# A two-layer attention block with less work ahead of its main loop: one place of maxima and two groups of queries moved

## The chip, the cores and the metric

The kernel runs on one core of a Trainium2 chip. The metric is the device time in microseconds of one execution, the median of several. A profiled execution of the same kernel gives the page and the trace that are read below. The engines are TensorE (PE; its weight load is listed as PEld), VectorE (DVE), ScalarE (ACT), GpSimd (POOL) and SyncE (SP), which here issues nearly all DMAs. Each engine works through its own instructions in order; they wait for each other by semaphores.

## The reference

All numbers are float32; one batch, S = 2048 rows, D = 512 columns, 32 query heads of 16 and a single head of keys and values:

```
mod = silu(c) @ w_mod                       # six rows of 512: sa, ca, ga, sb, cb, gb
h = layernorm(x) * (1 + ca) + sa
q = h @ wq  (32 heads of 16);  k = h @ wk;  v = h @ wv    # one head of k, v
p = softmax(q k^T / 4);  o = p v
x = x + ga * (o @ wo)
h = layernorm(x) * (1 + cb) + sb
out = x + gb * (relu(h @ w1) @ w2)          # w1: 512 x 1792, w2: 1792 x 512
```

The softmax is exact in form: the maximum of each row of scores is subtracted. The weights are scaled so that scores are large, and the matrix products are built from a rounded high part and a remainder where one rounded product isn't exact enough.

## The kernel before, in words

**Blocks, groups, units.** Rows of queries are handled in eight blocks of 256; the 32 heads in four groups of eight. A block and a group are a unit: 32 units, u = block * 4 + group. A unit's scores against all 2048 keys come in sixteen steps of 128 keys (`scores`, L723, with four tiles `ct` 0 to 3), each a matmul of 50 rows: 48 hold a head's queries and keys in high and low parts, the last two hold minus the row's maximum, high and low part, against rows of ones in `kp`. So a unit's scores can't be formed before its maxima are known and stand in those two rows. `values` (L847) multiplies the exponentials with the values; the sum of the exponentials comes along as another column.

**Maxima.** `max_of` (L417) forms 512 scores for 128 queries (L426) and VectorE reduces them (L428); there are 64 such for each unit, eight to a "place". After a unit's last one, VectorE reduces the four results a row (L432), turns them (L392), ScalarE and GpSimd split them (`split`, L239), SyncE writes them to DRAM in four DMAs (L399) and loads them in four others, one for each `ct`, into rows 48 and 49 of the unit's queries (L405).

**The head and the first loop (L794 to L828).** The first block of 512 rows of x is normalised and transposed, with the modulation's rows sa and ca; group 0 of the queries is formed (`qproj_now`, L803), written to DRAM in a layout of heads (L339) and loaded for unit 0 (`load_q`, L368, its DMAs at L376). Blocks of 512 are normalised in the order `ln1_sums` (L268: mean and variance), `ln1` (L273: the reciprocal root by VectorE in about 14 small operations, then the rows by GpSimd and ScalarE), `tr1` (L286: transposes, and the writes of `hT` with scale and shift) and `kv` (L302: keys and values). Then the first loop takes NBITS = 43 steps: in each, two or three maxima of those in `first_max`, and one step of the generator `first` (L653), which holds the rest of transposes, keys and values, queries of groups 1 and 2, and four modulation rows. `first_max` has the 64 maxima of unit 0 and LEAD / 8 = 3 places, 24 maxima, of unit 1. The constants NBITS and LEAD are written by hand.

**The main loop (L859 to L902).** 256 chunks, eight to a unit. The letters of PARTS (L40) give the order on TensorE in each chunk's two halves: `c` and `d` are scores (d is already of the next step, so that the first d of a unit stands in the second half of the chunk before it), `a` and `b` maxima of one place, `u` and `l` the two halves of a portion of other work on the other half of the array, `t` transposes; after each half the values. In a chunk the instructions are given out in this order: the letters; at position 3 of the first half what was put off (`put_off`: splits and their DMAs, among them L399); with the last `l` the next portion is fetched (`advance`), and whatever the generator does between two portions is issued there, its DMAs too; at the end what is due (`ends`: L405 among them) and a step of `chores` (loading and splitting weights, chunks 0 to 34).

The portions come from `queries` (L674: groups 3 to 13 of the sixteen products of 512 rows by 128 columns, three portions each) and then, block by block of 32 chunks, from `behind` (L511) for the block that is finished: rest of the second layer of the block before (7 portions for one half of the rows), projection, second norm, first layer in 14 portions with its weights loaded two ahead into three buffers `w1s` (L450, DMA L452), second layer. Finished rows go out by L533. In block 0, where no second layer is waiting yet, queries 14 and 15 and four empty portions stand in its place. An empty portion is filled with six matmuls whose result nobody reads (L873 to L876).

Where a place ends up in time: chunk c takes the place c + LEAD / 8 of those from unit 1 on. With three places ahead, the maxima of unit u end in chunk 8u - 4, L399 is issued in chunk 8u - 3 and L405 at that chunk's end; the first scores of unit u are in the second half of chunk 8u - 1. `load_q` of the next unit is issued when a unit has 16 maxima left (L421).

Of the kernel before, what the change touches and what calls it, by code (L numbers as in the profile page):

```python
# [9 lines left out]
F32 = mybir.dt.float32  # L10
F32R = mybir.dt.float32r
I32 = mybir.dt.int32
AF = mybir.ActivationFunctionType
OP = mybir.AluOpType
# [5 lines left out]
P = 128  # L20
LB = 512
NL = S // LB
TB = 256
# [4 lines left out]
NG = 4  # L28
# [2 lines left out]
NU = NB * NG  # L31
EPS = 1e-5
HP = 64
NBITS = 43
LEAD = 24
ET = mybir.EngineType


# [18 lines left out]
def build(tc, nc, cst, sb, ps, dr, x, wq, wk, wv, wo, w1, w2, c, w_mod, out):  # L57
# [21 lines left out]
    wm, xb1 = {}, {}  # L79
# [34 lines left out]
    cols = cst.tile([P, 2, DC], F32, name="cols")  # L114
# [7 lines left out]
    qdr = [[dr.tile([8, 48, LB], F32R, name=f"qdr{b}_{j}") for j in range(NG)] for b in range(NL)]  # L122
# [83 lines left out]
    def ln_sums(mv, t, src):  # L206
        st = sb.tile([P, 6], F32, name="st", tag="st", bufs=2)
        nc.vector.bn_stats(st, src)  # L208
        nc.vector.bn_aggr(mv[:, t], st)

    def ln_mv(n):
        return sb.tile([P, n, 2], F32, name="mv", tag="mv", bufs=2)

    def ln_stats(mv, n, late):
        nm = sb.tile([P, n], F32, name="nm", tag="nm", bufs=2)
        ve = sb.tile([P, n], F32, name="ve", tag="ve", bufs=2)
        y = sb.tile([P, n], F32, name="y", tag="y", bufs=2)
        u = sb.tile([P, n], F32, name="u", tag="u", bufs=2)
        yi = y.bitcast(I32)
        nc.vector.tensor_scalar(ve, mv[:, :, 1], EPS, None, op0=OP.add)  # L220
        nc.vector.tensor_scalar(yi, ve.bitcast(I32), 1, None, op0=OP.logical_shift_right)
        nc.vector.tensor_scalar(yi, yi, -1.0, float(0x5f3759df), op0=OP.mult, op1=OP.add)
        if late:
            for _ in range(3):
                nc.vector.tensor_tensor(u, y, y, op=OP.mult)
                nc.vector.scalar_tensor_tensor(u, u, -0.5, ve, op0=OP.mult, op1=OP.mult)
                nc.vector.scalar_tensor_tensor(y, u, 1.5, y, op0=OP.add, op1=OP.mult)
            nc.vector.tensor_scalar(nm, mv[:, :, 0], -1.0, None, op0=OP.mult)
            return nm, y
        nc.gpsimd.tensor_scalar(nm, mv[:, :, 0], -1.0, None, op0=OP.mult)  # L230
        for _ in range(3):
            nc.gpsimd.tensor_tensor(u, y, y, op=OP.mult)
            nc.gpsimd.tensor_tensor(u, u, ve, op=OP.mult)
            nc.gpsimd.tensor_scalar(u, u, -0.5, 1.5, op0=OP.mult, op1=OP.add)
            nc.gpsimd.tensor_tensor(y, y, u, op=OP.mult)
        return nm, y
# [28 lines left out]

    ln = {}

    def ln1_sums(b):  # L268
        ln[b] = ln_mv(4)
        for t in range(4):  # L270
            ln_sums(ln[b], t, xb1[b][:, t])

    def ln1(b):  # L273
        xb = xb1[b]
        nm, y = ln_stats(ln[b], 4, True)
        nmy = sb.tile([P, 4], F32, name="nmy", tag="nmy", bufs=2)
        nc.vector.tensor_tensor(nmy, nm, y, op=OP.mult)
        for t in range(4):
            if t < 2:
                nc.gpsimd.tensor_scalar(xb[:, t], xb[:, t], nm[:, t:t + 1], y[:, t:t + 1],  # L280
                                        op0=OP.add, op1=OP.mult)
            else:
                nc.scalar.activation(xb[:, t], xb[:, t], AF.Identity,
                                     bias=nmy[:, t:t + 1], scale=y[:, t:t + 1])

    def tr1(b):  # L286

        xb = xb1[b]
        h = hT[b] = sb.tile([P, DC, LB], F32, name="hT", tag="big", bufs=4)
        for k in range(DC):  # L290
            pt = ps_exp()
            for t in range(4):
                nc.tensor.transpose(pt[:, t * P:(t + 1) * P], xb[:, t, k * P:(k + 1) * P], idn)  # L293
            if b == 0 and k % 2:
                nc.vector.tensor_scalar(h[:, k], pt, cols[:, 1, k:k + 1], cols[:, 0, k:k + 1],
                                        op0=OP.mult, op1=OP.add)
            else:
                nc.scalar.activation(h[:, k], pt, AF.Identity,
                                     bias=cols[:, 0, k:k + 1], scale=cols[:, 1, k:k + 1])
            yield  # L300

    def kv(b):  # L302
# [26 lines left out]
    def qproj(b, j, bank, soon=False, qq=None):  # L329


        pt = bank()
        todo = [("f32", pt[:, n:n + TB], wqf[j][:, k], hT[b][:, k, n:n + TB],
                 n + k == 0, n + k == TB + DC - 1)
                for n in range(0, LB, TB) for k in range(DC)]

        def to_dram(qq):
            for r, part in ((0, 0), (32, 0), (16, 1)):
                nc.sync.dma_start(qdr[b][j].bitcast(F32)[:, r:r + 16], qq[:, part].bitcast(F32))  # L339

        def end():
            qt = qq if qq is not None else sb.tile([P, 2, LB], F32R, name="qq", tag="t4", bufs=2)
            if soon:
                nc.scalar.activation(qt[:, 0], pt, AF.Copy, scale=DH ** -0.5)
                nc.vector.scalar_tensor_tensor(qt[:, 1], pt, DH ** -0.5, qt[:, 0].bitcast(F32),
                                               op0=OP.mult, op1=OP.subtract)
                to_dram(qt)
                return
            stg = sb.tile([P, 512], F32, name="stg", tag="tmp", bufs=2)
            put_off.append(split_psum(qt[:, 0], qt[:, 1], pt, stg=stg, scale=DH ** -0.5))  # L350
            put_off.append(partial(to_dram, qt))

        return todo, end

    def qproj_now(*args):

        todo, end = qproj(*args)
        for n in range(0, len(todo), 2):
            on_all(todo[n])
            on_all(todo[n + 1])  # L360
            if n + 2 == len(todo):
                end()
            yield
# [4 lines left out]
    def load_q(u):  # L368
        b, g = divmod(u, NG)
        tb, to = divmod(b * TB, LB)  # L370
        qps[u] = []
        for i in range(2):
            t = sb.tile([P, 2, TB], F32R, name="qp", tag="qp", bufs=6)
            for hf in range(2):
                h0 = (i * 2 + hf) * 2
                nc.sync.dma_start(  # L376
                    t[hf * 64:hf * 64 + 48].bitcast(F32),
                    qdr[tb][g].bitcast(F32)[h0:h0 + 2, :, to:to + TB].rearrange("h r n -> r h n"))
            qps[u].append(t.rearrange("p a n -> p (a n)"))
# [37 lines left out]
    def max_of(u, hf, i, j, kb):  # L417
# [12 lines left out]
        if left[u] == 0:  # L430
# [9 lines left out]
                  for kb in range(KB) for hf in (1, 0)]  # L440
    places = places[LEAD // 8:]

# [68 lines left out]
    def behind(b):  # L511
# [23 lines left out]
        x1, oo = open_block(b)  # L535
        if b == 0:
            qqs = [sb.tile([P, 2, LB], F32R, name="qq", tag="w1s", bufs=3) for _ in range(2)]
            rest, fill = [others_of(14 + n, qqs[n]) for n in range(2)]
            fill = itertools.chain(fill, [[]] * 4)
        else:  # L540
            rest, fill = carried.pop(), second(b - 1, 1)
        yield next(rest)
# [5 lines left out]
        mv = ln_mv(TT)  # L548
        for t in range(TT):
            pt = ps_fill()  # L550
# [22 lines left out]
        for f2 in range(FC // 2):  # L573
            pt = ps_fill()
# [4 lines left out]
            i, f = divmod(f2 * 2, 8)  # L579
# [73 lines left out]
    def first():  # L653

        mods = [mod_all(i, dst, (ps_fill, ps_exp)[n % 2]) for n, (i, dst) in
                enumerate(((2, gr[:, 0]), (5, gr[:, 1]), (3, sbr), (4, cbr)))]
        yield from kvs[1]
        for b in range(2, NL):
            yield from trs[b]
            yield from kvs[b]  # L660
        yield from qproj_now(0, 1, ps_exp, True)
        load_q(1)
        for m in mods:
            yield from m
        yield from qproj_now(0, 2, ps_fill, True)

    def others_of(n, qq=None):

        todo, end = qproj(*divmod(n, NG), ps_fill, qq=qq)
        for i in range(0, len(todo), 3):  # L670
            yield todo[i:i + 3]
        end()

    def queries():  # L674
        for n in range(3, 14):
            yield from others_of(n)

    def chores():
# [106 lines left out]
    def run(g):  # L785
        for _ in g:
            pass
# [4 lines left out]
    kvs = [kv(b) for b in range(NL)]  # L792

    warm(32)  # L794
    ln1_sums(0)
    row1 = mod_row(1, ps_max())
    ln1(0)
    row0 = mod_row(0, ps_max())
    mod_col(row1, 1, True, ps_max())
    mod_col(row0, 0, False, ps_max())  # L800
    run(trs[0])
    ln1_sums(1)
    run(qproj_now(0, 0, ps_exp, True))  # L803
    ln1(1)
    load_q(0)
    for i in (2, 5, 3, 4):
        load_mod(i)
    for _ in range(DC):
        next(kvs[0])
    ln1_sums(2)  # L810
    run(trs[1])
    ln1(2)
    ln1_sums(3)
    next(kvs[0])
    for _ in range(DC):
        next(kvs[1])
    ln1(3)

    bits, done = first(), 1
    upto = [len(first_max) * n // NBITS for n in range(NBITS + 1)]  # L820
# [38 lines left out]
    for c in range(NU * KT // 2):  # L859
# [5 lines left out]
        if places:  # L865
            u, i, j = places.pop(0)
            todo_of.update(a=[partial(max_of, u, 0, i, j, kb) for kb in range(KB)],
                           b=[partial(max_of, u, 1, i, j, kb) for kb in range(KB)])
# [4 lines left out]
        if not portion:  # L873

            pt = ps_fill()
# [60 lines left out]
```

## Time and profile before

| what | us |
|---|---|
| median of three runs | 1703.93 |
| the three runs | 1693.88, 1703.93, 1709.46 |
| the profiled execution | 1703.82 |
| its span | 1702.0 |
| head, to the first reduce of a maximum | 41.09 |
| first scores of unit 0 | 109.77 |
| sum of unit 0 copied out | 159.11 |
| sum of unit 31 copied out | 1620.77 |

Times in a trace are counted from the start of the span. A row of the timeline has the start, the duration, the engine (a trailing q means its sequencer, which is where DMAs are issued), the line, the operation, what it writes and reads, and how many instructions were merged into the row; in brackets stands how long the engine was idle before it, and what ended that. The granted clock is TensorE's, as a share of full speed. "Busy" of TensorE is modelled in part, since matmuls are pipelined.

### The profile page before, as it was taken

The page shows a single profiled execution, that of the slowest core. Times are in us where ns is not written, and L with a number is a line of the kernel's source. Part 1 is how long each engine was busy: PE and PEld are TensorE (multiplying, and loading weights), DVE is VectorE, ACT ScalarE, POOL GpSimd, SP SyncE. Part 2 cuts the span into 40 slices and gives each one's busy share as a digit, 9 for nine tenths or more (in the row PEclk, how much of TensorE's full clock was granted, in tenths as well). Part 3 has the DMA queues.
Part 4 walks back from the last instruction along what each step waited for, and adds up shares of the span by engine and source line. Part 5 has one row for each costly group of instructions (what it writes and reads, how often), then busy time and mean ns, then how long its engine had stood idle before and what let it go on. Part 6 is the DMA issues. An engine that isn't in the chain of part 4 may idle for free.

```text
span 1702.0 us, 34026 instructions
## 1 busy us (share of the span) xinstructions
PE 1669.9 (98%) x13130; PEld 923.7 (54%) x13130; DVE 1374.6 (81%) x2347; ACT 1227.2 (72%) x2397; POOL 345.9 (20%) x434
## 2 busy tenths in 40 slices
PE   7999999999999999999999999999999999999988
PEld 5444444445654565546644565446644565456567
DVE  7788888888889888888889888888888888886031
ACT  4238888877877777778777787778877787778810
POOL 3103345331102211131113110131113110131110
PEclk9899999999999999999999999999999999999999
DMA  8024643212211131103201131103211230113133
GB/s 284 31 62 142 193 126 108 88 56 91 91 29 35 47 114 40 60 16 109 78 29 47 56 100 35 58 16 119 68 35 41 67 108 29 48 35 103 44 103 111
DMA packets 86928, 129.86 MB, mean 76 GB/s; under 512 B 25012, under 2 KB 52596, under 8 KB 86768
## 3 DMA queue, kind: packets, MB, share of 16 engines
q1 hardware_dynamic: 85184, 127.62, 24.2%
q8 instruction: 105, 1.72, 0.4%
q14 instruction: 55, 0.45, 0.1%
q10 hardware_dynamic: 1584, 0.07, 0.1%
HBM read 100.33 MB, written 25.15 MB: 74 GB/s over the span
## 4 chain that ended last, share of the span: by engine, by line
PE 93%; DVE 3%; DMA 2%; ACT 1%; issue 1%; POOL 0%; SPq 0%; POOLq 0%; DVEq 0%; ACTq 0%
PE ps_pv L853 30%; PE ps_exp L727 21%; PE ps_fill L163 19%; PE ps_max L426 18%; PE ps_exp L146 1%; PE ps_max L146 1%; DVE pm L428 1%; DMA w1s<-w1dr 1%; PE ps_exp L307 1%; DVE st L208 1%; PE ps_exp L293 0%; PE ps_exp L190 0%; DMA wmod<-in_w_mod_dram 0%; PE ps_exp L159 0%; PE ps_fill L190 0%
## 5 line engine op out<-in xcount | busy, mean ns | idle before, releaser
L428 DVE TENSOR_REDUCE pm<-ps_max 128x1 f32<-128x512 f32 x2048 | 1292.7, 684 | 189.6 <-PE ps_max L426 141.8
L729 ACT ACTIVATE pe<-ps_exp 128x512 f32<-128x512 f32 x2048 | 1081.2, 605 | 301.5 <-PE ps_fill L163 140.2
L426 PE MATMUL ps_max<-kp,qp 48*128 48x512 f32 x2048 | 805.1, 439 | 7.2 <-DVE pm L428 7.1
L727 PE MATMUL ps_exp<-qp,kp 50*128 50x512 f32 x2048 | 723.0, 412 | 1.9 <-ACT pe L729 1.8
L853 PE MATMUL ps_pv<-pe,vt 128*32 128x512 f32 x4096 | 545.5, 605 | 0.0
L426 PEld LDWEIGHTS ps_max<-kp,qp 48*128 48x128 f32 x2048 | 363.9, 185 | 264.7 <-DVE pm L428 237.4
L727 PEld LDWEIGHTS ps_exp<-qp,kp 50*128 50x128 f32 x2048 | 358.8, 185 | 269.1 <-ACT pe L729 177.9
L163 PE MATMUL ps_fill<-w2r,r 64*128 64x512 f32 x1044 | 302.7, 405 | 0.0
L163 PE MATMUL ps_fill<-hh,w1s 64*128 64x256 f32 x1568 | 243.1, 286 | 0.0
L163 PEld LDWEIGHTS ps_fill<-hh,w1s 64*128 64x128 f32 x1568 | 217.1, 186 | 12.9 <-PEq L156 6.7
L163 PEld LDWEIGHTS ps_fill<-w2r,r 64*128 64x128 f32 x1044 | 180.6, 185 | 11.8 <-PEq L156 2.5
L853 PEld LDWEIGHTS ps_pv<-pe,vt 128*32 128x32 f32 x4096 | 80.5, 108 | 142.3 <-issue 122.0
L163 PE MATMUL ps_fill<-hT,wq 64*128 64x256 f32 x416 | 128.3, 405 | 0.0
L241 POOL TENSOR_TENSOR r<-stg,r 128x512 fp32r<-128x512 f32 x49 | 62.9, 1283 | 322.1 <-ACT r L240 322.1
L163 PE MATMUL ps_fill<-hl,w1s 64*128 64x256 f32 x784 | 126.3, 280 | 0.0
L163 PEld LDWEIGHTS ps_fill<-hl,w1s 64*128 64x128 f32 x784 | 105.5, 185 | 0.0
L163 PEld LDWEIGHTS ps_fill<-hT,wq 64*128 64x128 f32 x416 | 68.3, 185 | 2.9
L897 POOL TENSOR_TENSOR on<-num,den 128x256 f32<-128x256 f32 x31 | 22.8, 736 | 231.2 <-DMA den<-recs 192.3
L743 POOL COPY num<-pvs 128x256 f32<-128x256 f32 x32 | 12.8, 398 | 179.4 <-ACT pvs L739 179.4
L241 POOL TENSOR_TENSOR hl<-stg,hh 128x512 fp32r<-128x512 f32 x14 | 18.0, 1284 | 131.3 <-ACT hh L240 131.3
L261 POOL TENSOR_TENSOR x<-stg,x 128x512 f32<-128x512 f32 x14 | 18.1, 1290 | 99.1 <-ACT stg L260 99.1
L248 ACT ACTIVATE stg<-ps_fill 128x512 f32<-128x512 f32 x62 | 38.2, 616 | 0.0
(139 smaller groups left out, 929.6 us busy)
## 6 DMA issues: line engine op xcount, KB each, us to landing
w1s<-w1dr SPq DMA_DIRECT2D x112, 512.0 KB
qdr<-qq SPq DMA_DIRECT2D x48, 256.0 KB
qp<-qdr SPq DMA_DIRECT2D x128, 96.0 KB
raw<-in_B_w_dram SPq DMA_DIRECT2D x28, 256.0 KB
w1dr<-w1s SPq DMA_DIRECT2D x14, 512.0 KB
wmod<-in_w_mod_dram SPq DMA_DIRECT2D x6, 1024.0 KB
x<-in_A_x_dram SPq DMA_DIRECT2D x8, 512.0 KB
out_dram<-ot SPq DMA_DIRECT2D x16, 256.0 KB
```

What stands on the lines that cost most here:

```text
L146: nc.tensor.matmul(pt, w, a, start=start, stop=stop)
L163: ins = nc.tensor.matmul(pt, w[r], a[r], start=start and h == 1, stop=stop and h == 0)
L208: nc.vector.bn_stats(st, src)
L241: (eng or nc.gpsimd).tensor_tensor(lo, src, hi.bitcast(F32), op=OP.subtract)
L248: nc.scalar.activation(stg, pt, func, **kw)
L261: nc.gpsimd.tensor_tensor(dst, stg, other, op=OP.add)
L426: nc.tensor.matmul(pt, qps[u][i][r, j * P:(j + 1) * P], kp[r, kb * 512:(kb + 1) * 512], start=True, stop=True)
L428: nc.vector.tensor_reduce(pms[u][:, (i * 2 + hf) * 4 + j, kb:kb + 1], pt, axis=AX.X, op=OP.max)
L727: nc.tensor.matmul(pt, kp[r, kt * P:(kt + 1) * P], qps[u][ct // 2][r], start=True, stop=True)
L729: nc.scalar.activation(pe, pt, AF.Exp)
L853: nc.tensor.matmul(pvt[i * 32:(i + 1) * 32], vt[:, kt], pes.pop((s, i)), start=(kt == 0), stop=(kt == KT - 1))
L897: due[1]()
```

## The change

Queries of group 1 (of the first 512 rows) are formed before the first loop and no longer in it, those of group 2 in the main loop, as the first of `queries`. Queries 11 move from `queries` to block 0 of `behind`, where they, 14 and 15 now leave one empty portion of four; 14 and 15 share one buffer. The first loop has 35 steps, and two places ahead, 80 maxima in all, 16 of unit 1. Queries formed early are written in two halves of columns, and the first half is loaded (`load_q`) before the second is written. The sums for blocks 1 to 3 stand earlier in the program, the statistics of blocks 2 and 3 are formed in one chain of operations on 8 columns, and all four writes of the first transposed block are by ScalarE. With two places ahead, the maxima of unit u end in chunk 8u - 3.

```diff
-NBITS = 43
-LEAD = 24
+NBITS = 35
+LEAD = 16
...
-    def ln1_sums(b):
-        ln[b] = ln_mv(4)
+    def ln1_sums(b, mv, n=0):
+        ln[b] = mv, n
         for t in range(4):
-            ln_sums(ln[b], t, xb1[b][:, t])
-
-    def ln1(b):
-        xb = xb1[b]
-        nm, y = ln_stats(ln[b], 4, True)
-        nmy = sb.tile([P, 4], F32, name="nmy", tag="nmy", bufs=2)
+            ln_sums(mv, n + t, xb1[b][:, t])
+
+    def ln1_stats(mv, n):
+        nm, y = ln_stats(mv, n, True)
+        nmy = sb.tile([P, n], F32, name="nmy", tag=f"nmy{n}", bufs=2)
         nc.vector.tensor_tensor(nmy, nm, y, op=OP.mult)
+        return nm, y, nmy
+
+    def ln1(b, nm, y, nmy):
+        xb, n = xb1[b], ln[b][1]
...
-            if b == 0 and k % 2:
-                nc.vector.tensor_scalar(h[:, k], pt, cols[:, 1, k:k + 1], cols[:, 0, k:k + 1],
-                                        op0=OP.mult, op1=OP.add)
-            else:
-                nc.scalar.activation(h[:, k], pt, AF.Identity,
-                                     bias=cols[:, 0, k:k + 1], scale=cols[:, 1, k:k + 1])
+            nc.scalar.activation(h[:, k], pt, AF.Identity,
+                                 bias=cols[:, 0, k:k + 1], scale=cols[:, 1, k:k + 1])
...
-        def to_dram(qq):
+        def to_dram(qq, cols=slice(0, LB)):
             for r, part in ((0, 0), (32, 0), (16, 1)):
-                nc.sync.dma_start(qdr[b][j].bitcast(F32)[:, r:r + 16], qq[:, part].bitcast(F32))
+                nc.sync.dma_start(qdr[b][j].bitcast(F32)[:, r:r + 16, cols],
+                                  qq[:, part, cols].bitcast(F32))
...
-                to_dram(qt)
+                to_dram(qt, slice(0, TB))
+                load_q(b * LB // TB * NG + j)
+                to_dram(qt, slice(TB, LB))
...
-            rest, fill = [others_of(14 + n, qqs[n]) for n in range(2)]
-            fill = itertools.chain(fill, [[]] * 4)
+            rest, *fill = [others_of(n, qqs[n > 11]) for n in (11, 14, 15)]
+            fill = itertools.chain(*fill, [[]])
...
-        yield from qproj_now(0, 1, ps_exp, True)
-        load_q(1)
         for m in mods:
             yield from m
-        yield from qproj_now(0, 2, ps_fill, True)
...
-        for n in range(3, 14):
+        for n in (*range(2, 11), 12, 13):
             yield from others_of(n)
...
     run(trs[0])
-    ln1_sums(1)
+    ln1_sums(1, mv[1])
+    stats1 = ln1_stats(mv[1], 4)
     run(qproj_now(0, 0, ps_exp, True))
-    ln1(1)
-    load_q(0)
+    ln1(1, *stats1)
     for i in (2, 5, 3, 4):
         load_mod(i)
     for _ in range(DC):
         next(kvs[0])
-    ln1_sums(2)
+    for b in (2, 3):
+        ln1_sums(b, mv[2], (b - 2) * 4)
     run(trs[1])
-    ln1(2)
-    ln1_sums(3)
     next(kvs[0])
+    stats23 = ln1_stats(mv[2], 8)
+    ln1(2, *stats23)
     for _ in range(DC):
         next(kvs[1])
-    ln1(3)
+    ln1(3, *stats23)
+    run(qproj_now(0, 1, ps_exp, True))
```

More of the change, by code (lines that the diff above doesn't have):

```diff
@@ L211, in ln_mv @@
     def ln_mv(n):
-        return sb.tile([P, n, 2], F32, name="mv", tag="mv", bufs=2)
+        return sb.tile([P, n, 2], F32, name="mv", tag=f"mv{n}", bufs=2)
     def ln_stats(mv, n, late):
[L215 to L218, printed above, removed]
+        nm = sb.tile([P, n], F32, name="nm", tag=f"nm{n}", bufs=2)
+        ve = sb.tile([P, n], F32, name="ve", tag=f"ve{n}", bufs=2)
+        y = sb.tile([P, n], F32, name="y", tag=f"y{n}", bufs=2)
+        u = sb.tile([P, n], F32, name="u", tag=f"u{n}", bufs=2)
         yi = y.bitcast(I32)
@@ L266, in build @@
     ln = {}
-    def ln1_sums(b):
-        ln[b] = ln_mv(4)
+    def ln1_sums(b, mv, n=0):
+        ln[b] = mv, n
         for t in range(4):
-            ln_sums(ln[b], t, xb1[b][:, t])
-    def ln1(b):
-        xb = xb1[b]
-        nm, y = ln_stats(ln[b], 4, True)
-        nmy = sb.tile([P, 4], F32, name="nmy", tag="nmy", bufs=2)
+            ln_sums(mv, n + t, xb1[b][:, t])
+    def ln1_stats(mv, n):
+        nm, y = ln_stats(mv, n, True)
+        nmy = sb.tile([P, n], F32, name="nmy", tag=f"nmy{n}", bufs=2)
         nc.vector.tensor_tensor(nmy, nm, y, op=OP.mult)
+        return nm, y, nmy
+    def ln1(b, nm, y, nmy):
+        xb, n = xb1[b], ln[b][1]
         for t in range(4):
+            one = slice(n + t, n + t + 1)
             if t < 2:
-                nc.gpsimd.tensor_scalar(xb[:, t], xb[:, t], nm[:, t:t + 1], y[:, t:t + 1],
+                nc.gpsimd.tensor_scalar(xb[:, t], xb[:, t], nm[:, one], y[:, one],
                                         op0=OP.add, op1=OP.mult)
@@ L283, in ln1 @@
                 nc.scalar.activation(xb[:, t], xb[:, t], AF.Identity,
-                                     bias=nmy[:, t:t + 1], scale=y[:, t:t + 1])
+                                     bias=nmy[:, one], scale=y[:, one])
     def tr1(b):
@@ L794, in build @@
     warm(32)
-    ln1_sums(0)
+    mv = [ln_mv(4), ln_mv(4), ln_mv(8)]
+    ln1_sums(0, mv[0])
     row1 = mod_row(1, ps_max())
-    ln1(0)
+    ln1(0, *ln1_stats(mv[0], 4))
     row0 = mod_row(0, ps_max())
```

## The prediction

> **What bounds the kernel now.** Read first the page's busy shares, then its chain that ended last, then the stages:
>
> ```profile
> PE 1669.9 (98%) x13130; PEld 923.7 (54%) x13130; DVE 1374.6 (81%) x2347; ACT 1227.2 (72%) x2397; POOL 345.9 (20%) x434
> PE 93%; DVE 3%; DMA 2%; ACT 1%; issue 1%; POOL 0%; SPq 0%; POOLq 0%; DVEq 0%; ACTq 0%
> 41.09:59.00 17.91, 17.18 (x39) 7.09 (x39) 11.47 (x20) 4.64 (x6) 1.52 (x2) 0.52 0.19 72
> 59.00:109.78 50.78, 50.04 (x168) 21.47 (x167) 45.12 (x76) 10.59 (x18) 5.31 (x5) 1.00 0.08 25
> 109.78:1561.00 1451.22, 1445.40 (x11933) 784.44 (x11933) 1267.21 (x2103) 1139.66 (x2241) 310.84 (x384) 1.00 0.24 71
> ```
>
> TensorE is the chain nearly everywhere. In the main loop (from 109.78) it is busy 1445.40 of 1451.22 us, so a pause put into its queue there lengthens the run by its own length. The first loop (41.09 to 109.78) is different: its first 18 us ran at a granted clock of 0.52. So two questions decide: what the first loop loses, and whether TensorE must wait in the main loop for something that now comes later.
>
> **The first loop.** Rows of the timeline, and one stage (its columns are the busy time of TensorE, its weight load, VectorE, ScalarE and GpSimd, then granted clock, DMA share and GB/s):
>
> ```profile
> 36.38 0.17 DVE L220 TENSOR_SCALAR ve<-mv 128x4 f32<-128x4 f32 x1
> 41.09 1.28 DVE L428 TENSOR_REDUCE pm<-ps_max 128x1 f32<-128x512 f32 x2
> 61.26 6.06 DVE L428 TENSOR_REDUCE pm<-ps_max 128x1 f32<-128x512 f32 x10
> 87.68 1.29 DVE L428 TENSOR_REDUCE pm<-ps_max 128x1 f32<-128x512 f32 x2 [0.19 <-PE ps_max L426]
> 110.51 0.69 DVE L345 SCALAR_TENSOR_TENSOR qq<-ps_fill,qq 128x512 fp32r<-128x512 f32 x1 [0.19 <-ACT qq L344]
> 109.77 0.96 PE L727 MATMUL ps_exp<-qp,kp 50*128 50x512 f32 x3
> 16.70 1.65 ACT L298 ACTIVATE hT<-ps_exp,cols 128x512 f32<-128x512 f32 x2 [1.18 <-PE ps_exp L293]
> 18.02 3.70 PE L146 MATMUL ps_exp<-hT,wq 128*128 128x256 f32 x16
> 31.71 5.35 PE L307 MATMUL ps_exp<-hT,wkv 128*128 128x512 f32 x8
> 38.50:41.91 3.41, 0.20 (x2) 0.09 (x1) 3.34 (x6) 1.44 (x3) 3.16 (x4) 1.00 1.05 387
> 22.38 2.06 SPq L339 DMA_DIRECT2D qdr<-qq  x3
> 29.93 1.76 SPq L376 DMA_DIRECT2D qp<-qdr  x4
> ```
>
> It ran 68.7 us, from the first maxima (41.09) to the first scores (109.77). A step with two maxima and two passes of 512 columns takes 1.29 + 0.19 = 1.48 us at full clock; a step of transposes is bound by its maxima, 6.06 / 5 = 1.2. After: 35 steps, 80 maxima, so ten steps have three. Those cost three reduces, 1.94. The sum: 8 steps of transposes (two of them with three maxima) 11.4; 3 short ones that turn the values 4; 24 others (eight with three) 39. That is 54.4, and 0.3 for the end of unit 0. VectorE alone would need 80 x 0.645 + 1 = 52.6, so 54.7 is no wild figure.
>
> Its start: the head loses one whole chain of norm statistics (some 14 small operations; the last chain held VectorE from 36.38 to 41.09) since blocks 2 and 3 share one, 8 wide at the same small price. It gains queries of group 1 in front of the loop: 3.70 us of TensorE. ScalarE takes over two of the first four writes of the transposed block, 0.83 each, which makes the first queries some 0.7 us later. Keys of block 1 then start at about 30.9 instead of 31.71, half of them at the lower clock as in the row of 5.35; they end at about 36.8, the queries at 40.5, their copy (0.6) and subtraction (0.69) at 41.8. First maxima at 41.8 against 41.09: +0.7, between -2 and +4 by how the clock stands. But TensorE now works from 31 to 41, where it was busy for 0.20 of the 3.41 us from 38.50, so I expect full clock in the loop. First scores at 41.8 + 54.7 = 96.5 against 109.77: **-13.3** (-9 to -17).
>
> The first exponentials then no longer queue behind the copy of group 2, nor its bank behind the subtraction at 110.51: **-0.7**. Writing the first queries in halves moves a load of q (it waited from 24.4 to 29.93 for the write to land) ahead of three more writes and of the four loads of modulation; each takes SyncE's queue about 2 us. These are hidden: q is first needed by the maxima at 41, and the modulation only after the keys of two more blocks. Without that cover it would cost those 2 us. Buffer tags per width cost nothing: memory, no instruction.
>
> **The main loop, without waits.** One place of eight maxima moves here. Ends of units (copy of the values' sum):
>
> ```profile
> 1435.79 0.60 ACT L739 ACTIVATE pvs<-ps_pv 128x512 f32<-128x512 f32 x1 [0.29 <-PE ps_pv L853]
> 1482.45 0.64 ACT L739 ACTIVATE pvs<-ps_pv 128x512 f32<-128x512 f32 x1
> 1576.94 0.60 ACT L739 ACTIVATE pvs<-ps_pv 128x512 f32<-128x512 f32 x1
> 1620.77 0.60 ACT L739 ACTIVATE pvs<-ps_pv 128x512 f32<-128x512 f32 x1 [3.01 <-PE ps_pv L853]
> ```
>
> A unit of eight chunks with maxima took 46.66, the last one, without, 43.83: 0.35 a place. Three portions of queries replace three of filler; no row prices the difference alone, so 0 to 1.0 (as if each were a place), and I take 0.35, near the lower end because both feed the same half of the array. Together **+0.7**.
>
> **The waits that appear.** A place less ahead means that each unit's maxima end one chunk (5.8 us, 46.66 / 8) later, while its scores stay where they are. The path: maxima, split, four writes to DRAM (L399), four loads (L405) into the queries, first scores. For unit 10:
>
> ```profile
> 573.52 1.70 SPq L399 DMA_DIRECT2D mdr<-ms  x4
> 576.37 1.13 SPq L405 DMA_DIRECT2D qp<-mdr  x4
> 583.52 0.36 SPq L533 DMA_DIRECT2D out_dram<-ot  x1
> 583.92 3.44 SPq L452 DMA_DIRECT2D w1s<-w1dr  x2
> 585.43 0.39 PE L727 MATMUL ps_exp<-qp,kp 50*128 50x512 f32 x1
> DMA  0000029999794787988995220000000969475889
> ```
>
> Before, L405 was issued 9.06 us before the unit's first scores (585.43). Shifted by 5.8, 3.2 remain; a 4 KB transfer lands about 1.5 after its issue (the last of the four writes goes out at about 574.8, and 576.37 waits for it), so where nothing else stands in SyncE's queue all is in time, with a microsecond to spare. But in the new chunk the finished rows (L533) and the first-layer weights (L452) are issued ahead of L405: the program fetches the next portion before it runs what is due. L405 then goes out from 584.3, and its packets stand behind 256 and 512 KB. The last line is the DMA engines' share in 40 slices of 0.15 us from 583.5: busy until slice 24, 587.1. So the load of ct 1 lands at about 587.6 and that of ct 3 at 588.1, where the scores want them at 585.43 and 0.23 later: 2.4 us. TensorE's queue is in order; values, maxima, fill and with them ScalarE and VectorE stand behind. The same place comes once in each block of four units: 10, 14, 18, 22, 26, 30. **+14.4** (0 if the chunk has slack that I don't see, 18 if DMA is slower).
>
> Units 1, 4 and 6 meet the write of queries (L339, 256 KB) instead:
>
> ```profile
> 239.40 2.94 SPq L339 DMA_DIRECT2D qdr<-qq  x3
> 242.43 2.42 SPq L399 DMA_DIRECT2D mdr<-ms  x4
> 247.04 1.43 SPq L405 DMA_DIRECT2D qp<-mdr  x4
> 149.49 2.36 SPq L339 DMA_DIRECT2D qdr<-qq  x3
> 156.38 0.39 PE L727 MATMUL ps_exp<-qp,kp 50*128 50x512 f32 x1
> 293.21 2.94 SPq L339 DMA_DIRECT2D qdr<-qq  x3
> 300.10 0.39 PE L727 MATMUL ps_exp<-qp,kp 50*128 50x512 f32 x1
> 390.00 1.28 POOL L241 TENSOR_TENSOR hl<-stg,hh 128x512 fp32r<-128x512 f32 x1 [5.16 <-ACT hh L240]
> 396.77 0.39 PE L727 MATMUL ps_exp<-qp,kp 50*128 50x512 f32 x1
> ```
>
> Unit 3 shows this meeting already: 4.7 us from the end of L339 (242.34) to L405, 1.2 to the last of its four, 1.5 to land. After, it moves to the chunks of units 1 and 4: 151.85 + 7.4 = 159.3 against 156.6, and 296.15 + 7.4 = 303.5 against 300.3. **+2.7** and **+3.2**. Unit 6: the last queries (15) are now split in the chunk of L399, behind the split at 390.00; written out by about 393.2, landed 5.5 later (as 24.4 to 29.93), and only then may the weights' load take their buffer and L405 follow: after 398.7 + 3 against 396.77: **+5** (2 to 7). The third queries themselves (read back a chunk after their write) have two microseconds to spare; 0 to +2, I take 0. Waits together: **+25.3**.
>
> **The clock.** Stages around low work:
>
> ```profile
> 24.84:28.26 3.42, 1.63 (x9) 0.89 (x8) 3.21 (x12) 2.61 (x5) 1.52 (x2) 1.00 0.51 187
> 1642.76:1646.17 3.41, 1.83 (x9) 1.23 (x7) 2.30 (x13) 0.00 (x0) 1.17 (x2) 1.00 0.00 0
> 1646.17:1649.59 3.42, 0.98 (x7) 0.74 (x7) 0.00 (x0) 0.58 (x2) 2.12 (x2) 1.00 0.21 77
> 1649.59:1653.00 3.41, 3.34 (x15) 3.34 (x16) 1.29 (x2) 0.51 (x2) 0.00 (x0) 0.50 0.00 0
> ```
>
> A stretch of 3.4 us with 0.98 busy was followed by one at 0.50, one with 1.83 was not; 1.63 (mostly transposes) was, as the keys' slow row shows. A pause of 2.4 leaves 1.0 of a stretch if it lies wholly within it, so some pauses will bring the half clock: I take five of the nine, one stretch each, 1.7 lost: **+8.5** (0 to 30; the slow stage at 41.09 lasted five stretches).
>
> [...]
>
> **Sum.** -13.3 - 0.7 + 0.7 + 25.3 + 8.5 = +20.5. The profiled execution took 1703.82 (span 1702.0), the median of the runs shown is 1703.93: **1725**.
>
> **Rivals.**
> [...]
> - No waits: if the loads of maxima pass in time (their order or size lets them overtake the 512 KB), the shorter first loop is all: 1703.8 - 13.3 = 1690.5, the other side. It decides at L405 landing by 585.4 in the chunk of unit 10; the DMA line, full to 587.1, speaks against.
> - The half clock lasts as at 41.09, five stretches, after four or so pauses: 4 x 8.5 in place of 8.5 gives 1750.
> - The head doesn't do what it should: the loop begins at half clock again, and gives 6 instead of 13.3: 1732.
>
> **Chances.** Forecast 0.38 (1718 to 1735), no half clock 0.27, no waits 0.10, long half clock 0.14, slow head 0.11. A measurement of this kernel tells about 1% from no change (its three runs lie 0.9% apart). Leaving out the no-waits case and the upper half of the long one gives 1704 to 1750. Within 1%, up to 1721: most of the second and third and a little of the first, 0.38; faster by more 0.04; slower by more 0.58.
>
> **What would show it.** First scores at about 96 us; no stretch at 0.5 after 42; L727 waiting for qp<-mdr with 2 to 5 us at units 1, 4, 6 and every fourth from 10; TensorE's clock at 0.5 in some of these. Wrong if L405 lands before the scores, or if unit 1's first chunks show other stalls than these.

## Result and the profile after

The changed kernel took **1727.88 us** (median of four; 1726.43 to 1734.64), the kernel before 1703.2: ratio **1.015, 95% interval 1.012 to 1.0179**. It is slower, by 1.5%. Its profiled execution took 1728.12, with a span of 1726.3 against 1702.0.

The lines of the changed kernel have moved: the maxima's writes are L402 (were L399), their loads L408 (L405), the first-layer weights' load L455 (L452), the maxima's reduction L431 (L428). L727, the scores, and L339, the queries' write, kept their numbers.

From the page of the changed kernel, the busy times, the chain by engine, and the group of the scores' matmuls (busy us, mean ns, idle before and its main releaser):

```profile
PE 1675.6 (97%) x13110; PEld 926.4 (54%) x13110; DVE 1365.5 (79%) x2330; ACT 1229.9 (71%) x2400; POOL 347.6 (20%) x435
...
PE 87%; DMA 4%; DVE 3%; ACT 2%; issue 1%; POOL 1%; SPq 1%; POOLq 0%; DVEq 0%; ACTq 0%
...
L727 PE MATMUL ps_exp<-qp,kp 50*128 50x512 f32 x2048 | 731.5, 416 | 24.8 <-DMA qp<-mdr 23.4
```

TensorE still ends the work, but its share of the chain fell from 93 to 87%, and the scores now stand idle 23.4 us for a DMA of maxima. By stages (from the first maxima to the first scores, from there to 1549.60, and on to the end of the last unit; the columns are length, busy of each engine, granted clock, DMA share, GB/s):

```profile
38.52:94.31 55.79, 54.21 (x165) 21.94 (x166) 50.26 (x86) 12.52 (x20) 5.79 (x6) 0.94 0.22 72
94.31:1549.60 1455.29, 1428.33 (x11616) 770.16 (x11615) 1238.83 (x2056) 1115.99 (x2192) 308.70 (x381) 0.99 0.23 68
1549.60:1643.90 94.30, 92.49 (x802) 54.30 (x803) 33.34 (x56) 74.21 (x146) 11.50 (x12) 1.00 0.23 71
```

The two traces, cut at first scores and at the end of the last unit:

| stage | before | after | difference |
|---|---|---|---|
| start to first scores | 109.77 | 94.31 | -15.5 |
| first scores to end of the last unit | 1511.0 (to 1620.77) | 1549.6 (to 1643.90) | +38.6 |
| rest | 81.2 | 82.4 | +1.2 |
| span | 1702.0 | 1726.3 | +24.3 |

So the head and the first loop gave what was wanted of them, and the main loop lost two and a half times as much. Where it lost is shown, in TensorE's timeline, by the first scores of units 1, 6, 10, 14 and 18 (start, time; in brackets the idle time before and its releaser); units 4, 22, 26 and 30 have such a wait too, of 2.42, 2.33, 2.20 and 2.19 us, and no other unit has one:

```profile
144.00 0.79 PE L727 MATMUL ps_exp<-qp,kp 50*128 50x512 f32 x1 [2.92 <-DMA qp<-mdr]
...
396.35 0.73 PE L727 MATMUL ps_exp<-qp,kp 50*128 50x512 f32 x1 [4.08 <-DMA qp<-mdr]
...
588.63 0.49 PE L727 MATMUL ps_exp<-qp,kp 50*128 50x512 f32 x1 [2.02 <-DMA qp<-mdr]
...
780.62 0.49 PE L727 MATMUL ps_exp<-qp,kp 50*128 50x512 f32 x1 [3.05 <-DMA qp<-mdr]
...
973.08 0.63 PE L727 MATMUL ps_exp<-qp,kp 50*128 50x512 f32 x1 [2.17 <-DMA qp<-mdr]
```

Why they wait is in SyncE's queue, here in the chunk of unit 10 of the changed kernel (start, time, issues):

```profile
581.21 1.71 SPq L402 DMA_DIRECT2D mdr<-ms  x4
584.54 0.36 SPq L536 DMA_DIRECT2D out_dram<-ot  x1
584.95 0.43 SPq L455 DMA_DIRECT2D w1s<-w1dr  x1
585.55 1.15 SPq L408 DMA_DIRECT2D qp<-mdr  x4
```

Before, L405 stood ahead of the finished rows (L533) and the weights (L452) by 7 us; now the four 4 KB loads go out behind them, and the scores start 3.1 us after the first load's issue (588.63 - 585.55), 2.02 of it idle.

The rest of the loss is TensorE's clock. In this trace the granted clock is 1.00 or 0.50, and it changes on a grid of 3.41 us: the first and the last of the stretches at half clock after the pauses begin at 143.86 and 1359.01, 1215.15 us or 356 steps apart. The two grid stretches that touch the pauses of units 10, 14 and 18:

```profile
584.18:587.59 3.41, 2.43 (x25) 1.25 (x21) 2.82 (x5) 1.68 (x4) 0.34 (x1) 1.00 0.64 193
587.59:591.01 3.42, 2.38 (x25) 1.67 (x25) 1.16 (x2) 1.86 (x4) 0.00 (x0) 1.00 0.11 42
...
775.33:778.74 3.41, 2.24 (x22) 1.06 (x18) 2.63 (x5) 1.49 (x4) 0.18 (x1) 1.00 0.53 127
778.74:782.15 3.41, 1.53 (x16) 1.37 (x17) 0.32 (x1) 1.00 (x3) 0.00 (x0) 1.00 0.29 113
...
969.89:973.30 3.41, 1.24 (x13) 0.52 (x6) 1.41 (x3) 0.27 (x1) 0.00 (x0) 1.00 0.62 214
973.30:976.71 3.41, 3.41 (x21) 2.45 (x23) 1.89 (x3) 2.27 (x4) 0.00 (x0) 0.50 0.02 5
```

The number right behind the length is TensorE's busy time. Unit 18's pause lay wholly in one stretch, which held 1.24 us of work, and the next was granted 0.50. Unit 10's pause, almost as long, fell across a boundary, left 2.43 and 2.38 in the two stretches, and cost no clock. Of the nine pauses seven were followed by half clock, in eight stretches in all (two after unit 1); those of units 10 and 30 were not.

### The profile page after: what moved, and what is told of

It reads as the page before. It is cut to its first block, busy times and chain, and to the rows that moved or that the text cites. A ratio compares the mean times of both kernels' runs of the same rounds, so it can differ in the third digit from the quotient of the medians.

```text
span 1726.3 us, 33964 instructions
## 1 busy us (share of the span) xinstructions
PE 1675.6 (97%) x13110; PEld 926.4 (54%) x13110; DVE 1365.5 (79%) x2330; ACT 1229.9 (71%) x2400; POOL 347.6 (20%) x435
## 3 DMA queue, kind: packets, MB, share of 16 engines
q1 hardware_dynamic: 86000, 127.62, 24.3%
## 4 chain that ended last, share of the span: by engine, by line
PE 87%; DMA 4%; DVE 3%; ACT 2%; issue 1%; POOL 1%; SPq 1%; POOLq 0%; DVEq 0%; ACTq 0%
PE ps_pv L856 28%; PE ps_exp L727 21%; PE ps_max L429 17%; PE ps_fill L163 16%; DVE pm L431 1%; DMA qp<-mdr 1%; PE ps_max L146 1%; DMA w1s<-w1dr 1%; PE ps_exp L146 1%; ACT pe L729 1%; DVE st L208 1%; DMA xb<-in_A_x_dram 1%; PE ps_exp L307 1%; PE ps_fill L190 0%; PE ps_exp L190 0%
## 5 line engine op out<-in xcount | busy, mean ns | idle before, releaser
L431 DVE TENSOR_REDUCE pm<-ps_max 128x1 f32<-128x512 f32 x2048 | 1292.3, 683 | 223.0 <-PE ps_max L429 204.8
L727 PE MATMUL ps_exp<-qp,kp 50*128 50x512 f32 x2048 | 731.5, 416 | 24.8 <-DMA qp<-mdr 23.4
L727 PEld LDWEIGHTS ps_exp<-qp,kp 50*128 50x128 f32 x2048 | 360.4, 186 | 303.4 <-ACT pe L729 173.6
L429 PEld LDWEIGHTS ps_max<-kp,qp 48*128 48x128 f32 x2048 | 368.4, 186 | 263.2 <-DVE pm L431 233.6
L163 PE MATMUL ps_fill<-hT,wq 64*128 64x256 f32 x448 | 140.2, 411 | 0.0
L163 PEld LDWEIGHTS ps_fill<-hT,wq 64*128 64x128 f32 x448 | 75.1, 189 | 2.9
```

The lines of the kernel that those rows point to most:

```text
L163: ins = nc.tensor.matmul(pt, w[r], a[r], start=start and h == 1, stop=stop and h == 0)
L429: nc.tensor.matmul(pt, qps[u][i][r, j * P:(j + 1) * P], kp[r, kb * 512:(kb + 1) * 512], start=True, stop=True)
L431: nc.vector.tensor_reduce(pms[u][:, (i * 2 + hf) * 4 + j, kb:kb + 1], pt, axis=AX.X, op=OP.max)
L727: nc.tensor.matmul(pt, kp[r, kt * P:(kt + 1) * P], qps[u][ct // 2][r], start=True, stop=True)
```

## Experiments

**The theory**: a place less of lead makes the loads of maxima late behind larger transfers, and the pauses lower TensorE's clock. **Its rivals**: the loss does not hang on where the loads stand in SyncE's queue; or the pauses cost only their own length, and the clock nothing; or the loss comes from the queries that were moved, not from the lead. In some of the expectations they go by letters, with the numbers that each would give.

### Early loads

```diff
         for parts, load in later:
             put_off.append(parts)
-            ends.append((c, load))
+            loads.append(load)
 ...
             for n, what in enumerate(PARTS[part]):
+                if part == 1 and n == 13:
+                    in_turn(loads)
+                    loads.clear()
```

> The changed kernel, with the four loads of the maxima (L408) issued in a chunk's second half ahead of the fetch of the next portion, so ahead of the finished rows and of the first-layer weights in SyncE's queue; every instruction and every byte is the same. Theory (queue): of the 23.4 us in which TensorE waited for these loads, the six waits of units 10 to 30 (14.0) and that of unit 6 (4.1) go, with their six or so half-clock stretches (1.7 each); units 1 and 4 keep 2.9 and 2.4. So about 1728 - 18 - 10 = 1700. Rival A (the place itself is too late, wherever the loads stand): at most 3 us better, above 1724. Rival B (what is now issued later, the weights, makes TensorE wait instead): above 1715.

Measured: 1706.6 us, ratio to before 1.0018 (0.9985 to 1.0052). In the chunk of unit 10 the order is now the reverse of that above:

```profile
583.34 1.70 SPq L402 DMA_DIRECT2D mdr<-ms  x4
586.10 1.12 SPq L408 DMA_DIRECT2D qp<-mdr  x4
587.27 0.36 SPq L536 DMA_DIRECT2D out_dram<-ot  x1
587.67 2.79 SPq L455 DMA_DIRECT2D w1s<-w1dr  x2
```

All six waits from unit 10 on are gone, and with them their stretches at half clock: every unit from 8 on is back within 0.3 us of its length before, but for two near the end, 0.7 and 0.3 longer. What is left of the waits on TensorE (us in all, times, longest) is almost all (8.0) at units 1, 4 and 6, the ones that meet the queries' write:

```profile
PE ps_exp L727 <- DMA qp<-mdr: 8.5, 5, 2.8
```

So the place in the queue makes those six waits. The run came out 6.6 above the 1700 expected. The waits of units 1 and 4 were expected to stay; that of unit 6 should have gone and kept 2.8 of its 4.1 us, and four stretches at half clock stayed where some two were expected.

### Both orders

The same, and the split of the maxima and their writes run ahead of the queries' split and write:

```diff
         for parts, load in later:
-            put_off.append(parts)
+            put_off.insert(0, parts)
```

> As the run with early loads, and in addition the split of the maxima and their four writes go ahead of the other things put off, so ahead of the write of queries in the chunks of units 1, 4 and 6. Theory (queue): no wait for the maxima's loads is left, no half clock in the main loop; only the shorter head stays: 1728 - 23 - 14 = 1691 (1686 to 1697), below the kernel before. Rival A (place too late): above 1720. Rival C (the moved queries cost more than 0.7 in the loop): waits gone, but the time stays at 1700 or above.

Measured: 1708.11 us, 1.0005 (0.9976 to 1.0035): a miss. The order is as wished, and the waits stay, 8.2 us in three, at units 1, 4 and 6. SyncE's queue in the chunk of unit 1:

```profile
135.45 1.73 SPq L402 DMA_DIRECT2D mdr<-ms  x4
137.28 1.99 SPq L339 DMA_DIRECT2D qdr<-qq  x3
139.45 1.39 SPq L408 DMA_DIRECT2D qp<-mdr  x4
```

And TensorE's first scores of that unit, with the idle time ahead of them:

```profile
144.61 0.49 PE L727 MATMUL ps_exp<-qp,kp 50*128 50x512 f32 x1 [2.20 <-DMA qp<-mdr]
```

The loads are issued by 140.84, 1.6 us before the scores want them (144.61 - 2.20 = 142.41), and yet the scores start 5.2 us after the first load's issue. They are no longer late in SyncE's queue, as they were in the changed kernel, which issued them from 142.21 where the scores wanted them at 141.08 (144.00 - 2.92). But L339 was issued between the maxima's writes and their loads, and it is three transfers of 256 KB each, 768 KB in all.

### Loads first

The queries' write is kept back until the loads are issued:

```diff
-            put_off.append(partial(to_dram, qt))
+            late.append(partial(to_dram, qt))
 ...
                 if part == 1 and n == 13:
                     in_turn(loads)
                     loads.clear()
+                    in_turn(late)
+                    late.clear()
```

(In a chunk without loads, it stays where it was.)

> The changed kernel with the maxima written first, their loads (L408) issued at the same early place as in the early-loads kernel, and the third queries' group written to DRAM (L339, 256 KB) only after those loads. All work is kept. My theory (where a queries' group is written in the chunk, the 4 KB loads land late because the 256 KB stand ahead of them, in SyncE's queue or in the DMA engines): the three waits at units 1, 4 and 6 (8.2 us in the kernel with both orders) go, to under 1 us in all; so do the three half-clock stretches beside them; from the 1702.9-us span of the kernel with both orders that is 8 us of waits and some 1.7 us each for three stretches: 1689, as a time some 1691 (1686 to 1698). Rival (the landing at these units is set by the maxima's own write, L402, and not by what lies between): the 8 us stay, 1703 to 1708. Second rival (the queries written later now hold up their own load a chunk later): a wait of the maxima's matmuls on qp from qdr appears at units 1, 4 and 6, 1700 or more.

Measured: **1695.69 us, 0.9936 (0.9904 to 0.9968)**, faster than the kernel before. SyncE's queue in the chunk of unit 1, to set beside the one just shown:

```profile
136.70 1.72 SPq L402 DMA_DIRECT2D mdr<-ms  x4
139.57 1.13 SPq L408 DMA_DIRECT2D qp<-mdr  x4
140.74 1.97 SPq L339 DMA_DIRECT2D qdr<-qq  x3
```

The loads go out at nearly the same time as in the kernel with both orders, 139.57 against 139.45, and no wait of the scores for them is left anywhere. What differs is whether the 768 KB go ahead: that settles the second cause as something behind SyncE's queue, since loads that were issued in time come late. That their packets stand behind the large write's in the DMA engines is inferred from the order of issue; the trace doesn't say which packet is whose. The rival that the maxima's own writes set the landing fell: L402 went out 1.25 us later here than there. The rival that the queries would then be late fell too: no wait on queries appears. One new stall does: 1.9 us on ScalarE's exponentials in unit 1, followed by one stretch at half clock, which makes that unit 51.3 us in place of 48.0. The chain of work shows the fetch of a raw weight tile (4.39 us of it) just ahead; I tried nothing on it.

### Busy pauses

The changed kernel with unread matmuls put where it waits:

```diff
+    idle_of = {8: 10, 32: 8, 48: 14, **{u * 8: 7 for u in range(10, NU, 4)}}
 ...
+                if part == 1 and n == 3 and c + 1 in idle_of:
+                    pt = ps_max()
+                    for k in range(idle_of[c + 1]):
+                        nc.tensor.matmul(pt, kp[:, 0:P], kp[:, 0:512], start=True, stop=True)
```

> The changed kernel with matmuls that nobody reads placed in the nine pauses, just before the first scores of units 1, 4, 6, 10, 14, 18, 22, 26, 30 (10, 8, 14 and then 7 each of 512 columns, some 0.22 us each): the wait for the loads stays as long, but TensorE works through most of it. Theory (pauses bring the half clock): the half-clock stretches of the main loop go, 8 in the changed kernel's trace, about 1.7 each, so 1728 - 13 = 1715 (1711 to 1720), with the waits for the loads shown short and the matmuls in their place. Rival D (the half clock comes by itself, or by the kind of work): as many stretches as before and 1726 or above.

Measured: 1720.19 us, 1.0092 (1.006 to 1.0124), so 7.7 below the changed kernel, 0.2 above the expected range (1711 to 1720) and below the 1726 of rival D. The idle time left for maxima is 4.1 us (9 times, longest 0.9), and no stretch of the main loop is at half clock, eight before. From first scores to the last unit's end (granted clock 1.00):

```profile
96.84:1635.42 1538.58, 1528.09 (x12492) 831.38 (x12492) 1273.11 (x2111) 1189.56 (x2337) 319.70 (x393) 1.00 0.22 69
```

The main loop is 11.0 us shorter than the changed kernel's 1549.6, though it runs 74 matmuls more. That is a lower bound of what the half clock costs; the upper one is what the waits leave of the loss, 38.6 - 23.4 = 15.2. Eight stretches at half of 3.41, 13.7, lie between. Some 2.5 us of the gain were lost again ahead of the loop, where the first scores came at 96.84 in place of 94.31. So it was the pauses that brought the half clock here: eight stretches with them, none once they were filled.

### Lead alone

The kernel before, with one constant changed:

```diff
-LEAD = 24
+LEAD = 16
```

> The kernel before with only one number changed: two places of maxima ahead instead of three (LEAD 16), still 43 steps in the first loop, all else as before. Theory (queue): waits at units 1, 4 and every fourth from 10 (unit 6 hardly, since its queries were written earlier there), 19 us, with six or seven half-clock stretches (11), and some 1 us gained in the first loop: 1703 + 29 = 1732 (1725 to 1738), above the changed kernel, because the better head is missing. Rival E (the waits belong to the moved queries, not to the lead): below 1712.

Measured: 1737.06 us, 1.0158 (1.0104 to 1.0212). The waits come with the lead and without the moved group:

```profile
PE ps_exp L727 <- DMA qp<-mdr: 16.2, 10, 2.5
```

Six stretches of its main loop are at half clock (mean granted clock there 0.99, 1.00 in the kernel before). So the rival that the moved queries make the loss fell. The time is 5 us above the 1732 expected; the first loop ran a further 13.7 us at half clock (from 61.6), and the first scores came at 113.41, later than the 109.77 of before although one place, eight maxima, fewer comes ahead of them. That I had not expected.

### Three places

The changed kernel with the old lead, and block 0's third queries back in the first loop:

```diff
-NBITS = 35
-LEAD = 16
+NBITS = 39
+LEAD = 24
 ...
+        yield from qproj_now(0, 2, ps_fill, True)
```

> The changed kernel with LEAD back at 24 and the third queries' group of block 0 back in the first loop: the changes of the head (sums, half-written queries) and the order of the second group stay, the lead of the maxima is the old one. Theory (the loss is the short lead alone, the gain that of the head): no wait for qp from mdr over 1 us, no half-clock stretch in the main loop, first scores some 6 us later than in the changed kernel, since sixteen matmuls and eight more rows of maxima return to the first loop; loop as before: some 1692 (1686 to 1699), faster than before by 4 to 17 us. Rival (the head's gain of the changed kernel came from the group that left the first loop, not from the sums): first scores at 105 us or later, total within 3 us of before, 1700 to 1706.

Measured: **1696.33 us, 0.9961 (0.9928 to 0.9995)**. Its first loop and its main loop:

```profile
38.20:101.07 62.87, 61.29 (x189) 26.01 (x189) 55.27 (x94) 13.10 (x21) 5.80 (x6) 0.92 0.15 51
101.07:1611.50 1510.43, 1504.38 (x12414) 815.90 (x12414) 1268.22 (x2104) 1187.45 (x2335) 318.19 (x392) 1.00 0.23 71
```

The main loop is that of before (1510.43 against 1511.0), with no wait for maxima and no half clock. The first scores come 8.7 us earlier than before, at 101.07, and 6.8 later than in the changed kernel. So of the 15.5 us gained ahead of the loop, some 8.7 are the sums, the half-written queries and the new place of group 1, and some 6.8 the group that left with the shorter lead (either takes in what the clock did in that execution). The rival, that the gain was the group's alone, fell.

### Maxima first

The changed kernel with only the writes (`put_off.insert(0, parts)`) moved ahead, the loads left at the end of the chunk.

> The changed kernel, except that the split of the maxima and its four writes (L402) go out ahead of the steps that wait at the same place (queries' split and write, the other splits); the loads (L408) stay at the end of the chunk. Theory (the loads are issued too late at the end of the chunk, whatever the writes do): the six waits at units 10, 14 to 30 stay, 12 to 15 us in all, and the time stays within 6 us of the changed kernel, 1722 to 1730. Rival (it is the writes that are late, behind the other split on VectorE or the queries' write on SyncE): waits under 8 us in all, 1712 or less.

Measured, in one execution: 1735.35 us, and

```profile
PE ps_exp L727 <- DMA qp<-mdr: 25.3, 9, 5.6
```

The waits are not fewer (23.4 in the changed kernel), and the six from unit 10 on are 13.3 us, as expected: earlier writes help nothing while the loads go out late. The time is 5 us above the expected range: the mean granted clock of this execution was 0.982, against 0.988 in the changed kernel's profiled one, and the first scores came at 102.85, 8.5 us later than there.

### Busy head

Since the first loop's half clock changed from kernel to kernel with the same head, four unread matmuls were put into its longest pause, in the kernel with the loads first:

```diff
+            if upto[n] + k == 3:
+                pt = ps_fill()
+                for _ in range(4):
+                    nc.tensor.matmul(pt, kp[:, 0:P], kp[:, 0:512], start=True, stop=True)
             max_of(*m)
```

> The kernel with the loads first, plus four unread matmuls on the keys of block 1 just ahead of the first loop's fourth product of maxima, where TensorE waits 1.4 us for the maxima's buffer (L429 on DVE pm L431). No work is left out. Theory (this pause brings the half clock that stands at 40.7 for 13.7 us in the kernel with the loads first, at 41.5 for 6.8 us in the changed one, and 13.7 us of it cost some 5 us): no half-clock stretch between 38 and 60 us, first scores at 91 to 93 us in place of 96.8, the rest as before: some 1691 (1685 to 1696), 0.985 to 0.993 of the kernel before. Rival (the half clock there comes from the transposes that fill the stretch, not from the 1.4-us pause): it stays for 6.8 us or more, first scores at 95 or later, 1695 to 1700.

Measured: 1692.32 us, 0.9939 (0.992 to 0.9958), which can't be told from the kernel with the loads first. Its profiled execution contradicts the reason for the forecast. These are three stretches of the grid there:

```profile
51.39:54.80 3.41, 2.99 (x17) 1.81 (x16) 3.34 (x7) 2.62 (x5) 2.41 (x2) 1.00 0.18 56
54.80:58.22 3.42, 3.42 (x13) 1.87 (x11) 2.55 (x5) 1.55 (x2) 0.13 (x1) 0.50 0.00 0
61.63:65.04 3.41, 3.41 (x7) 0.98 (x6) 1.29 (x2) 0.00 (x0) 0.00 (x0) 0.50 0.00 0
```

The stretch at 40.7 is gone, as the theory had it, but the clock fell at 54.80, after a stretch with 2.99 of 3.41 us busy and no pause over 0.32, and stayed at half for 30.7 us, first scores at 104.10. Each theory has a part: with the pause filled the early stretch is gone, and a late one came with no pause over 0.32 us before it. This is one of ten executions, at a mean granted clock of 0.988; eight of the ten had 0.993 to 0.998, so a late stretch of this length isn't in most of them.

## Why the prediction came out

**Sum.** 1725 forecast, 1727.88 measured; +20.5 forecast against the profiled span, +24.3 measured. Term by term:

| term | forecast | measured |
|---|---|---|
| first loop and head | -13.3 | -15.5 |
| first exponentials | -0.7 | not seen by itself; unit 0, from its first scores on, took 49.34 before and 49.41 in the loads-first kernel |
| main loop without waits | +0.7 | not seen by itself; 1514.04 in the loads-first kernel, with some 3.6 of the new stall and its half clock in it, 1511.0 before |
| six waits from unit 10 | +14.4 | 13.96 |
| unit 1, unit 4, unit 6 | +2.7, +3.2, +5 | 2.92, 2.42, 4.08 |
| half clock of the pauses | +8.5 | 11.0 to 15.2 |
| tail | 0 | +1.2 (half clock there for 6.8 us, 3.4 before) |

**The waits were right in place, cause and size**: 25.3 forecast, 23.4 measured, in exactly the nine units named. The early loads and the loads-first kernel show both causes, each for its own units: the order of issue at 10 to 30, the queries' write between writes and loads at 1, 4 and 6 (at 6 the order of issue was worth 1.3 of the 4.08 us as well). For units 1 and 4 the prediction had put it down to L408 being issued late behind L339 in SyncE's queue; the kernel with both orders shows that issuing in time was not enough. That step was right in size and only half of its cause. It also gave L339 as 256 KB, which is one of its three transfers; the write is 768 KB.

**The clock was mis-sized.** Five of nine pauses with one stretch each were taken; seven did it, in eight stretches. The prediction had it that a pause must lie within one stretch; what it lacked was the place of each pause on the grid. Of the stretches at full clock around the nine pauses, those followed by half clock held at most 1.89 us of work, those not followed at least 2.24. A 2.2-us pause leaves 1.2 when it lies in one stretch, and is shared out when it straddles two. These numbers are no limit: a stretch with 2.20 us of work was followed by half clock (38.05 to 41.46 of the changed kernel), and three with 1.65, 1.82 and 1.83 were not (from 11.18, 1629.10 and 1642.76 in the kernel before). At six units pauses of 2.17 to 3.05 us, with 0.6 to 1.9 us of work in the stretch, were followed by half clock. The case of no half clock, 0.27 of the chances, fell with that, and the kernel with busy pauses shows it.

**The first loop was right in sum, wrong in one row.** First maxima came at 38.52 in place of 41.8, as the keys of block 1 started at 29.46, 1.4 ahead of the forecast, and lost their half clock:

```profile
29.46 3.70 PE L307 MATMUL ps_exp<-hT,wkv 128*128 128x512 f32 x8 [0.24 <-ACT hT L298]
41.46:48.29 6.83, 6.83 (x19) 3.19 (x17) 5.32 (x9) 2.33 (x3) 0.00 (x0) 0.50 0.57 200
```

The first row took 5.35 before. But the forecast "no stretch at 0.5 after 42" was wrong: the second row is one, and in other kernels with this head it is 13.7 us long (40.66 to 54.32 with the loads first) and 30.7 (54.80 to 85.52 with the busy head). That 94.31 came out below 96.5 is partly luck: this execution had a short one.

**The rivals.** "No waits" (1690.5) did not happen, but its price was near: the loads-first kernel, which has the moved work and none of these waits, took 1694.75 in its profiled execution. "Long half clock" (1750) did not happen in the main loop: each stretch there ended after one or two. Of "slow head" (1732) the condition came true in part, since the first loop was at half clock again from 41.46, but for 6.8 us only and without the loss. Its price is borne out elsewhere: in the kernel with maxima first, at a mean granted clock of 0.982, the first scores came 6.9 us ahead of the kernel before (102.85 against 109.77), against the 6 of this rival.

## What to carry over

When a buffer's lead is cut, work out for each place of the loop what is issued between the small transfer and its reader, on the queue and in the DMA engines, and not the slack alone: here 3.2 us of slack against 1.5 us of landing was enough in most units and too little in the nine where 512 or 768 KB stood ahead. The cure was to issue the small loads ahead of the big transfers, which kept the shorter lead and its gain; moving the lead back did as well. And a short wait of TensorE is to be priced with the clock it may cost: here 23 us of waits brought 11 to 15 us more.

## What the runs showed of the hardware

- **A 4 KB load issued in time was late behind a large write.** In the chunk of unit 1 with nearly the same issue time (139.45 and 139.57), the scores waited 2.20 us with three transfers of 256 KB ahead and not at all without.
- **Half clock after a stretch that the profile calls busy.** The stretch of 51.39 in the last kernel was 2.99 us busy, 0.90 of it in transposes (L297, 128 x 128) and 0.43 in the small ones of L322. The stretch after it was at 0.50. A share of transposes alone doesn't tell such a stretch: in the changed kernel the one from 24.39 to 27.81, 2.00 us busy with 1.53 of it in such transposes (L297), was followed by full clock. So why the clock fell at 54.80 stays open.
- **How long it lasted stays open too.** In the main loop of the changed kernel six of the seven pauses with half clock had one such stretch of 3.41 us, busy throughout; at unit 1, where the pause reached into it and left 3.28 of 3.42 us busy, a second followed. In the first loop it took two to nine stretches (6.8 to 30.7 us), nearly all of them fully busy and some without any transpose, as the one from 61.63. The first scores moved with it: 94.31 at 6.8 us (the changed kernel) and 96.84 at 13.7 (loads first), some 0.4 us for each us at half clock. Executions of one and the same program differ in this as well: in the 18 of the kernel before that were measured beside the loads-first kernel, the span goes from 1692.6 us at a mean granted clock of 0.997 to 1714.0 at 0.984.
